# Half-height transposes and a permutation matrix in an attention plus Fourier-mixing kernel on one Trainium2 core

## The chip, the cores and the metric

The kernel runs on one core of one Trainium2 chip. The metric is the device time of one execution in microseconds, the median of several runs. A core has five engines with a queue each: TensorE (PE in the profile; its weight loads are shown apart as PEld), VectorE (DVE), ScalarE (ACT), GpSimd (POOL) and SyncE (SP, which here issues nearly all DMAs). TensorE writes only to PSUM, eight banks of 2 KB in each of 128 partitions; DVE and ACT copy results from there to SBUF.

## The reference

All numbers are 32-bit floats. Two blocks follow each other. The first is linear attention with random features for 8 batches, 8 heads, 576 tokens, head width 64 and 128 features:

```python
def phi(x):
    proj = np.einsum('bhsd,md->bhsm', x, omega)
    sq = np.sum(x * x, axis=-1, keepdims=True) / 2.0
    h = proj - sq
    h = h - np.max(h, axis=-1, keepdims=True)
    return np.exp(h) / np.sqrt(m)
q_p, k_p = (phi(q_s), phi(k_s))
kv = np.einsum('bhsm,bhsd->bhmd', k_p, v)
z = np.sum(k_p, axis=2)
num = np.einsum('bhsm,bhmd->bhsd', q_p, kv)
den = np.einsum('bhsm,bhm->bhs', q_p, z)[..., None] + 1e-06
```

(`num / den` is its result.) The second block takes it as x, 8 x 576 x 512:

```python
X = np.fft.fft(x, axis=1)
X = np.fft.fft(X, axis=2)
mixed = np.real(X).astype(np.float32)
u = x + mixed
mu = np.mean(u, axis=-1, keepdims=True)
var = np.mean((u - mu) ** 2, axis=-1, keepdims=True)
un = (u - mu) / np.sqrt(var + 1e-06)
ch = np.maximum(un @ w_ch1, 0.0) @ w_ch2
return (u + ch).astype(np.float32)
```

## The kernel before, in words

**Two stages.** The first stage does attention, the Fourier mixing of each batch, the conversion of the 64-bit weights to 32-bit floats (`narrow`, L444 to L462), and sums of weight blocks for a Strassen-like scheme (L1326). The second does the two large products, L1501 and L1954, with sums of blocks around them; its first parts (L1658) already run beside the end of the first.

**Attention.** The 64 heads of all batches are taken as 32 pairs, four pairs a batch. Three streams run over the pairs (`pairs`, each takes every third), so that up to three pairs are under way. For one pair (`attn`):

1. The keys and then the queries of two heads are loaded, each 288 KB, to one tile `kq` (L383 and L386). There are two such tiles.
2. `transposed` turns them into `kqT`: nine 128x128 blocks, j = 0 to 8, the first four and a half of which hold keys. Each is one TensorE transpose against the identity (L519). They go in groups of four, four and one, each group to one PSUM bank, and one copy moves a group to SBUF (`evicted`: L535 on ACT or L533 on DVE).
3. `pairs_of` multiplies `kqT` with the random features (L613), for blocks 0 to 3, block 4, and blocks 5 to 8, each time to two neighbouring banks. The first six pairs (`NWIDE`) use tiles of 64 rows and 128 columns, the others tiles of 64 by 64.
4. `softmax` takes the negated maximum on DVE (L556) and the exponential on ACT (L573, 128 columns an instruction, 18 a pair), to tiles `e`. A bank comes free when its last exponential is done.
5. Key features times values give kv (L647, tiles of 64 by 64), kept in SBUF by L661 or L663.
6. `transposed` turns the nine blocks of query features into `qeT` (L519 again), in groups of one, four and four (`ORDER_R` gives the order of the blocks). The copy out of PSUM also moves columns to where the mixing wants its tokens: two copies a group, each reading a strided pattern, six a pair.
7. `qeT` times kv gives numerator and denominator (L694, L702, tiles of 128 rows and 64 columns); DVE forms the reciprocal (L711, L712), and L723 (DVE) or L719 (ACT) the quotient, into one of two token tiles `x`.

**Mixing.** When a batch's four pairs are in `x`, `mix` folds them on DVE or POOL (L750 to L786), multiplies with cosine and sine tables (L806, L816, L856, L867), adds the result to `x` (L913 to L933) and stores `u` to DRAM.

**The order of the work.** Nothing is in the order of the program text. Each piece of work is a `Step` with the engines that may run it and the time that it is thought to take on each; a `Listing` plays the streams forward and always places the step that can begin first on its engine, with small preferences (`bias`). It is greedy; nothing is searched or given by hand. It keeps track of PSUM banks: a step takes a "bank" (one) or a "duo" (two neighbouring ones, an even number first). A step on PE has a `mode`, the tile shape ("whole", "rows", "quarters", "halves"); where it differs from that of the step before, the listing adds 0.12 us. The list that comes out is the order of each engine's queue, and an engine works through its queue in that order, waiting where it must. A whole transpose is priced 0.109 us.

Of the kernel before, what the change touches and what calls it, by code (L numbers as in the profile page):

```python
# [18 lines left out]
F32 = mybir.dt.float32  # L19
# [268 lines left out]
def kernel(  # L288
# [10 lines left out]
    nc = tc.nc  # L299

    B, H, S, D = q.shape
# [14 lines left out]
    R = S // 64  # L316
# [30 lines left out]
    ident = const.tile([128, 128], F32, name="ident")  # L347
# [3 lines left out]
    fix = early.enter_context(tc.tile_pool(name="fix", bufs=1))  # L351
# [7 lines left out]
        kq=NKQ, turned=NS, e=NE, e1=NS, kv=NS, x0=1, x1=1, fold=1, half=1, y=1,  # L359
# [3 lines left out]
    def psum_of(b):  # L363

        i = b.ids[0]
        return banks[:, i] if len(b.ids) == 1 else banks[:, i : i + 2]

    def got():

        return listing.got, psum_of(listing.got)  # L370
# [35 lines left out]
    nc.gpsimd.memset(mhalf[:], -0.5)  # L406
    w2 = hids.tile([128, NFC, DM], F32, name="w2", tag="hid")
    om2 = fix.tile([128, MF], F32, name="om2")


    vds += [fix.tile([P, R, D + 1], F32, name=f"vd{i}") for i in range(NV)]
# [90 lines left out]
    def transposed(src, name, groups, after, makes, give, order=None):  # L502


        dst = None
        for j0, j1 in groups:
            m = j1 - j0
            yield Step(
                PE,
                0.109 * m,  # L510
                after=after(j0, j1),
                take=("bank",) + (("turned",) if j0 == 0 else ()),
                give=give(j0, j1), bias=0.14,
            )
            if dst is None:
                dst = att.tile([128, R, 128], F32, name=name, tag="turned")
            b, ps = got()
            for j in range(j0, j1):
                nc.tensor.transpose(ps[:, (j - j0) * 128 : (j - j0 + 1) * 128], src(j), ident[:])  # L519
            yield Fork(evicted(dst, b, j0, j1, makes, order))  # L520
        return dst

    def evicted(dst, b, j0, j1, makes, order):
        cost = (0.13 + 0.1 * (j1 - j0)) if order else 0.05 + 0.107 * (j1 - j0)
        step = Step(
            {ACT: cost, DVE: 0.06 + 0.133 * (j1 - j0) + (0.06 if order else 0.0)}, late=0.02,
            makes=makes + (j0,), give=(b,), bias=0.08,
        )
        yield step

        def copy(out, in_):
            if step.eng == DVE:
                nc.vector.tensor_copy(out=out, in_=in_)  # L533
            else:
                nc.scalar.activation(out=out, in_=in_, func=AF.Copy)  # L535

        ps = psum_of(b)[:, 0 : 128 * (j1 - j0)].rearrange("q (c p) -> q c p", p=128)
        dst = dst[:, j0:j1, :]
        if order is None:
            copy(dst, ps)  # L540
            return
        h, s, t = order[j0]
        dst = dst.rearrange("q c p -> q (c p)").rearrange("q (h s t c) -> q s h t c", h=h, s=s, t=t)
        ps = ps.rearrange("q c (h t s) -> q s h t c", h=h, s=s)
        for i in range(s):
            of = ps[:, i, :, ::-1, ::-1] if i and j0 else ps[:, i]
            copy(dst[:, i], of)
# [32 lines left out]
    def attn(n):  # L580
        b, pr = divmod(n, NP)

        yield Step(NONE, after=(("k", n),) + ((("vd", n - 1),) if n else ()))
        kq = kqs.pop(n)

        flat = kq[:].rearrange("p c d -> p (c d)")
        kqT = yield from transposed(
            lambda j: flat[:, 128 * j : 128 * j + 128],
            "kqT",
            ((0, 4), (4, 8), (8, R)),  # L590
            lambda j0, j1: (("kq", n),) if j1 > 4 else (),
            ("kqT", n),
            lambda j0, j1: ("kq",) if j1 == R else (),
        )
# [35 lines left out]
        def feature(c):  # L630
# [7 lines left out]
            mode="quarters",  # L638
            after=tuple(("e", n, t) for t in range(3)) + (("vd", n),),
            take=("duo",),  # L640
            give=("e", "e", f"vd{n % NV}"), bias=-0.19,
        )
        kvb, kvp = got()
        for r in range(R):
            for i, h in ((0, 0), (1, 1), (0, 1), (1, 0)):
                rows, cols = slice(D * i, D * i + D), slice(D * h, D * h + D)
# [9 lines left out]
        def keep():  # L656
# [8 lines left out]

        yield Fork(keep())
        qeT = yield from transposed(
            lambda j: feature(R + ORDER_R[j]),
            "qeT",
            ((0, 1), (1, 5), (5, R)),  # L670
            lambda j0, j1: tuple(
                ("e", n, t) for t in sorted({place(R + ORDER_R[j])[0] for j in range(j0, j1)})
            ),
            ("qeT", n),
            lambda j0, j1: {1: ("e1",), 5: (), R: ("e", "e")}[j1],
            {0: (2, 2, 32), 1: (4, 2, 16), 5: (4, 2, 16)},
        )
        yield Step(
# [2 lines left out]
            mode="halves",  # L681
            after=(("kv", n), ("qeT", n, 0), ("qeT", n, 1), ("qeT", n, 5)),
            take=("duo",),
            give=("turned", "kv"), bias=0.12,
# [23 lines left out]
        x = xts[b % 2]  # L708
# [4 lines left out]
        dst = x[:, :, 2 * D * pr : 2 * D * (pr + 1)].rearrange("p c (i d) -> p i c d", i=2)  # L713
        step = Step({DVE: 0.74, ACT: 1.97}, give=(ndb,), makes=("x", b, pr), bias=-0.07)
        yield step
        if step.eng == ACT:
            for i in range(2):
                for c in range(5):
                    nc.scalar.activation(  # L719
                        out=dst[:, i, c], in_=nd[:, i, c, 0:D], func=AF.Copy, scale=rden[:, i, c : c + 1]  # L720
# [3 lines left out]
            out=dst,  # L724
# [270 lines left out]
    turned = {}  # L995
# [421 lines left out]
    def pairs(start):  # L1417
        for n in range(start, B * NP, NS):
            yield from attn(n)
# [770 lines left out]
```

## Time and profile before

| | |
|---|---|
| Time, median of 3 runs (lowest to highest) | 1223.65 us (1218.25 to 1226.66) |
| Time of the profiled execution | 1219.09 us |
| Its span in the profile | 1217.3 us |
| Mean granted clock of TensorE | 0.965 |
| PE, share of the span busy | 92% |
| DVE | 80% |
| ACT | 48% |
| POOL | 23% |

The profile is one execution, taken by the hardware. A line of a group names the line of the kernel, the engine, the operation, what is written and read with shapes (128\*64 is a TensorE tile of 128 rows and 64 columns), the count, the time busy in us with the mean of one in ns, and the idle time just before, with what ended it. A record's length on PE and ACT holds the instruction's latency, so in a row of the same kind the distance from start to start is shorter than the mean, and that distance is what one of them costs. The chain of waits goes back from the last instruction, at each step to what released it, or to the one before it on its engine.

### The profile page before, as it was taken

The numbers are of one execution on the slowest core, as the hardware profiler recorded it, in microseconds if no ns is written. First come the engines' busy times: TensorE is split into PE (matmuls) and PEld (weight loads), VectorE is DVE, ScalarE is ACT, GpSimd is POOL, SyncE is SP. The second block draws the span as 40 slices with busy tenths as digits, with TensorE's granted clock in tenths as the row PEclk, the third lists the DMA queues.
The fourth block names the chain that finished last, engine by engine and source line by source line (L and its number), as shares of the span: only waits on it lengthen the run. The fifth ranks groups of instructions, "written<-read, shape, count | busy, mean of one in ns | idle before, by whom it ended". The sixth has DMA issues, their size and how long they took to land.

```text
span 1217.3 us, 32303 instructions
## 1 busy us (share of the span) xinstructions
PE 1121.6 (92%) x12571; PEld 1034.9 (85%) x12571; DVE 974.1 (80%) x1788; ACT 582.1 (48%) x1795; POOL 276.5 (23%) x292
## 2 busy tenths in 40 slices
PE   8888987987579698999998999999999999999998
PEld 7776876876467588999998988999988999988998
DVE  6998999997878767777877687888867799757895
ACT  7867967967484183261253256322355222332221
POOL 2231332321010120032054125500036400044000
PEclk9998998998798799999999899999999999999999
DMA  9745845848743599898879877875776865757453
GB/s 250 228 143 152 246 119 173 244 136 267 235 162 101 155 312 288 259 288 276 271 224 272 280 245 204 263 202 157 236 210 202 262 183 176 211 150 225 134 156 110
DMA packets 209656, 255.83 MB, mean 210 GB/s; under 512 B 55264, under 2 KB 125152, under 8 KB 209504
## 3 DMA queue, kind: packets, MB, share of 16 engines
q1 hardware_dynamic: 209008, 253.50, 68.4%
q8 instruction: 100, 1.64, 0.6%
q14 instruction: 52, 0.43, 0.1%
q10 hardware_dynamic: 496, 0.26, 0.1%
HBM read 200.74 MB, written 57.15 MB: 212 GB/s over the span
## 4 chain that ended last, share of the span: by engine, by line
PE 76%; DVE 9%; ACT 8%; DMA 5%; issue 1%; SPq 0%; POOL 0%; DVEq 0%; ACTq 0%
PE banks L1954 31%; PE banks L1501 26%; ACT e L573 5%; PE banks L1658 4%; PE banks L613 4%; PE banks L647 3%; PE banks L519 3%; PE banks L694 2%; PE banks L806 2%; DVE nmx L556 2%; DMA wl<-w2l 2%; PE banks L816 1%; DMA raw<-in_moe_w_ch_dram 1%; DVE x L933 1%; ACT qeT L535 1%
## 5 line engine op out<-in xcount | busy, mean ns | idle before, releaser
L1954 PE MATMUL banks<-wl,sums 128*128 128x128 f32 x2016 | 250.4, 278 | 0.7 <-DMA wl<-w2l 0.5
L1954 PEld LDWEIGHTS banks<-wl,sums 128*128 128x128 f32 x2016 | 240.4, 195 | 1.6 <-issue 1.0
L573 ACT ACTIVATE e<-banks,nmx 128x128 f32<-128x128 f32 x576 | 159.3, 443 | 32.7 <-DVE nmx L556 32.7
L1954 PE MATMUL banks<-wl,hid 128*128 128x128 f32 x936 | 122.0, 278 | 8.7 <-DMA wl<-w2l 8.3
L1954 PEld LDWEIGHTS banks<-wl,hid 128*128 128x128 f32 x936 | 113.8, 194 | 9.9 <-issue 4.7
L613 PE MATMUL banks<-om,kqT 64*64 64x128 f32 (+1 forms) x2088 | 91.0, 295 | 29.9 <-ACT e L573 23.7
L613 PEld LDWEIGHTS banks<-om,kqT 64*64 64x64 f32 (+1 forms) x2088 | 75.7, 151 | 41.6 <-ACT e L573 29.3
L556 DVE TENSOR_REDUCE nmx<-banks 128x8 f32<-128x1024 f32 (+1 forms) x96 | 87.3, 951 | 20.4 <-PE banks L613 12.9
L1925 ACT ACTIVATE s<-banks 128x128 f32<-128x128 f32 x126 | 34.9, 277 | 132.9 <-PE banks L1954 116.4
L1501 PE MATMUL banks<-unw,wxw 128*128 128x256 f32 x352 | 85.5, 379 | 0.0
L1954 PE MATMUL banks<-wl,hx 128*128 128x128 f32 x576 | 74.3, 275 | 0.4 <-DVE part L1930 0.4
L1501 PEld LDWEIGHTS banks<-unw,wxw 128*128 128x128 f32 x352 | 66.5, 190 | 8.8
L1930 DVE TENSOR_TENSOR part<-banks,s 128x128 f32<-128x128 f32 x114 | 33.0, 290 | 49.6 <-PE banks L1954 44.4
L1501 PE MATMUL banks<-rx,wxw 128*128 128x256 f32 x288 | 71.1, 379 | 0.0
L1526 ACT ACTIVATE s<-banks 128x512 f32<-128x512 f32 x72 | 42.6, 595 | 57.9 <-PE banks L1501 52.2
L1501 PE MATMUL banks<-ttw,wxw 128*128 128x256 f32 x288 | 70.0, 379 | 0.0
L1954 PEld LDWEIGHTS banks<-wl,hx 128*128 128x128 f32 x576 | 69.4, 192 | 0.7 <-DVE part L1930 0.6
L462 POOL TENSOR_TENSOR w<-w,raw 128x512 f32<-128x512 f32 x30 | 41.4, 1379 | 124.9 <-DVE raw L456 110.3
L1501 PEld LDWEIGHTS banks<-rx,wxw 128*128 128x128 f32 x288 | 54.5, 190 | 7.3
L1501 PEld LDWEIGHTS banks<-ttw,wxw 128*128 128x128 f32 x288 | 54.5, 190 | 7.3
L519 PE MATMUL banks<-ident,kq 128*128 128x128 f32 x288 | 44.8, 296 | 17.0 <-ACT e L573 10.9
L1970 ACT ACTIVATE banks<-banks 128x128 f32<-128x128 f32 x63 | 16.6, 263 | 86.3 <-PE banks L1954 83.9
(244 smaller groups left out, 2398.0 us busy)
## 6 DMA issues: line engine op xcount, KB each, us to landing
wl<-w2l SPq DMA_DIRECT2D x294, 256.0 KB, 3.6
wxw<-w1x SPq DMA_DIRECT2D x120, 256.0 KB, 3.2
raw<-in_moe_w_ch_dram SPq DMA_DIRECT2D x32, 512.0 KB, 5.2
kq<-in_k_dram SPq DMA_DIRECT2D x32, 288.0 KB, 4.0
kq<-in_q_dram SPq DMA_DIRECT2D x32, 288.0 KB, 4.2
vd<-in_v_dram SPq DMA_DIRECT2D x32, 288.0 KB, 4.6
wx<-w1x SPq DMA_DIRECT2D x36, 256.0 KB, 3.3
u<-us SPq DMA_DIRECT2D x128, 64.0 KB, 3.1
```

The source lines that it names most:

```text
L462: eng.tensor_tensor(out=dst, in0=dst, in1=lof, op=ALU.add)
L519: nc.tensor.transpose(ps[:, (j - j0) * 128 : (j - j0 + 1) * 128], src(j), ident[:])
L556: nc.vector.tensor_reduce(nmx[:, :, 0:num], pps[:, :, 0 : MF * num].rearrange("p b (c m) -> p b c m", m=MF), axis=AX.X, op=ALU.max, negate ...
L573: nc.scalar.activation(out=e[:, c + (i if num == 1 else 0), :], in_=pps[:, i, MF * c : MF * c + MF], func=AF.Exp, bias=nmx[:, i, c : c + 1],)
L613: nc.tensor.matmul(pps[cols, c, MF * m : MF * m + MF], lhsT=kqT[rows, j, cols], rhs=om2[rows, :],)
L647: nc.tensor.matmul(kvp[cols, i, 0 : D + 1], lhsT=feature(r)[rows, cols], rhs=vds[n % NV][rows, r, :], start=(r == 0), stop=(r == R - 1),)
L1501: nc.tensor.matmul(ps[:, span * f : span * f + span].rearrange("f (b q) -> f b q", q=Q), lhsT=left[:, P * f : P * f + P], rhs=right, start ...
L1526: nc.scalar.activation(out=s[:], in_=ps, func=AF.Copy)
L1658: nc.tensor.matmul(cell.rearrange("f t (b q) -> f t b q", q=Q), lhsT=w[:, d, col : col + 128], rhs=right[:, :, d].rearrange("f (t b) q -> ...
L1925: nc.scalar.activation(out=s[:], in_=ps[:, 0:128], func=AF.Copy)
L1930: nc.vector.tensor_tensor(out=part[:, t, 128 * m : 128 * m + 128], in0=ps[:, 0:128], in1=saved[with_][:], op=ALU.add,)
L1954: nc.tensor.matmul(ps[:, 0:128], lhsT=left[:, f], rhs=wls[head(j), i, n][:, f], start=start and f == 0, stop=(f == 3), skip_group_check=True,)
```

## The change

In both kinds of transposes eight blocks of nine are done as two half-height tiles each: rows 0 to 63 and rows 64 to 127 of a block are transposed apart, by TensorE tiles of 64 rows, to two neighbouring banks. The ninth stays whole. For this, the steps of a kind are grouped as `(((0, 4), (4, 8)), ((8, R),))`, so the first eight are one step on PE, with mode "rows", priced 0.07 a block, that takes a duo. Its two copies out of PSUM stand in one stream, one behind the other, where before each group's copy was a stream of its own; the duo is given back after the second. The first step of `kqT` now waits for keys and queries, where it waited for the keys alone.

For the query features the identity is replaced by a permutation matrix `perm`, loaded once from DRAM on ACT's queue, and the matmul's output columns are written with strides, so that the columns land in PSUM already in the order wanted. Three plain copies a pair, of 512, 512 and 128 columns, replace the six strided ones.

The diff, without the parts that only rename or regroup:

```diff
+    perm = fix.tile([128, 2, 128], F32, name="perm")
...
+    nc.scalar.dma_start(perm[:], nc.inline_tensor(np.ascontiguousarray(moved_to), name="k_perm").ap())
...
-        for j0, j1 in groups:
+        for parts in groups:
+            j0, j1 = parts[0][0], parts[-1][1]
             m = j1 - j0
+            split = len(parts) > 1
             yield Step(
                 PE,
-                0.109 * m,
+                (0.07 if split else 0.109) * m,
+                mode="rows" if split else "whole",
                 after=after(j0, j1),
-                take=("bank",) + (("turned",) if j0 == 0 else ()),
+                take=("duo" if split else "bank",) + (("turned",) if j0 == 0 else ()),
                 give=give(j0, j1), bias=0.14,
             )
...
+                if order:
+                    i, n = j - j0, (j - j0) // 4
+                    if not split:
+                        nc.tensor.transpose(ps[:, 0:128], src(j), perm[:, 0, :])
+                        continue
+                    for r in range(2):
+                        rows = slice(D * r, D * r + D)
+                        c = i % 4
+                        step_ = 67 - 2 * c
+                        out = ps[:, r, :]
+                        out = bass.AP(out.tensor, out.offset + 256 * n + c, [list(out.ap[0]), [128, 2], [step_, 2], [4, 16]])
+                        nc.tensor.transpose(out, src(j)[rows, :], perm[rows, 1, rows])
+                    continue
+                if split:
+                    for r in range(2):
+                        rows = slice(D * r, D * r + D)
+                        nc.tensor.transpose(
+                            ps[:, r, (j - j0) * D : (j - j0 + 1) * D], src(j)[rows, :], ident[rows, rows]
+                        )
+                    continue
                 nc.tensor.transpose(ps[:, (j - j0) * 128 : (j - j0 + 1) * 128], src(j), ident[:])
-            yield Fork(evicted(dst, b, j0, j1, makes, order))
+            yield Fork(evicted(dst, b, parts, makes, order))
...
+    def evicted(dst, b, parts, makes, order):
+        for j0, j1 in parts:
+            yield from copied(dst, b, j0, j1, parts, makes, order)
...
-            makes=makes + (j0,), give=(b,), bias=0.08,
+            makes=makes + (j0,), give=(b,) if j1 == parts[-1][1] else (), bias=0.08,
...
+        if order and split:
+            k0 = D * (j0 - parts[0][0])
+            copy(dst.rearrange("q c p -> q (c p)").rearrange("q (r x) -> q r x", r=2), psum_of(b)[:, :, k0 : k0 + 256])
+            return
+        if order:
+            copy(dst[:, 0, :], psum_of(b)[:, 0:128])
+            return
+        if split:
+            k0 = D * (j0 - parts[0][0])
+            ps = psum_of(b)[:, :, k0 : k0 + D * (j1 - j0)].rearrange("q r (c p) -> q c r p", p=D)
+            copy(dst.rearrange("q c (r p) -> q c r p", r=2), ps)
+            return
...
-            ((0, 4), (4, 8), (8, R)),
-            lambda j0, j1: (("kq", n),) if j1 > 4 else (),
+            (((0, 4), (4, 8)), ((8, R),)),
+            lambda j0, j1: (("kq", n),),
...
-            ((0, 1), (1, 5), (5, R)),
+            (((0, 1),), ((1, 5), (5, R))),
```

More of the change, by code (lines that the diff above doesn't have):

```diff
@@ L408 @@
     om2 = fix.tile([128, MF], F32, name="om2")
+    perm = fix.tile([128, 2, 128], F32, name="perm")
+    h_, s_, t_ = np.meshgrid(np.arange(2), np.arange(2), np.arange(32), indexing="ij")
+    told = [(h_ * 64 + t_ * 2 + s_).ravel()]
+    h_, s_, t_ = np.meshgrid(np.arange(4), np.arange(2), np.arange(16), indexing="ij")
+    told.append((h_ * 32 + np.where(s_ == 1, 15 - t_, t_) * 2 + s_).ravel())
+    moved_to = np.stack([np.eye(128, dtype=np.float32)[:, o] for o in told], axis=1)
+    nc.scalar.dma_start(perm[:], nc.inline_tensor(np.ascontiguousarray(moved_to), name="k_perm").ap())
     vds += [fix.tile([P, R, D + 1], F32, name=f"vd{i}") for i in range(NV)]
@@ L518, in transposed, with copied @@
             for j in range(j0, j1):
+                if order:
[18 more added lines that the diff above has]
+                    continue
                 nc.tensor.transpose(ps[:, (j - j0) * 128 : (j - j0 + 1) * 128], src(j), ident[:])
-            yield Fork(evicted(dst, b, j0, j1, makes, order))
+            yield Fork(evicted(dst, b, parts, makes, order))
         return dst
-    def evicted(dst, b, j0, j1, makes, order):
+    def evicted(dst, b, parts, makes, order):
+        for j0, j1 in parts:
+            yield from copied(dst, b, j0, j1, parts, makes, order)
+    def copied(dst, b, j0, j1, parts, makes, order):
+        split = len(parts) > 1
         cost = (0.13 + 0.1 * (j1 - j0)) if order else 0.05 + 0.107 * (j1 - j0)
@@ L535, in copy @@
                 nc.scalar.activation(out=out, in_=in_, func=AF.Copy)
+        dst = dst[:, j0:j1, :]
+        if order and split:
[10 more added lines that the diff above has]
+            return
         ps = psum_of(b)[:, 0 : 128 * (j1 - j0)].rearrange("q (c p) -> q c p", p=128)
-        dst = dst[:, j0:j1, :]
         if order is None:
@@ L674, in attn @@
             ("qeT", n),
-            lambda j0, j1: {1: ("e1",), 5: (), R: ("e", "e")}[j1],
+            lambda j0, j1: {1: ("e1",), R: ("e", "e")}[j1],
             {0: (2, 2, 32), 1: (4, 2, 16), 5: (4, 2, 16)},
```

## The prediction

> **What bounds the kernel now.** I read the page first (busy shares, slices), then the table by stage, then the chain of waits up to 412 us, the waits of the same stretch, and last single records of the transposes in the timeline.
>
> The table by stage, cut where the last attention and mixing work ends (columns: length, PE, PEld, DVE, ACT, POOL busy with counts, granted clock, DMA share, GB/s):
>
> ```profile
> 0.00:412.00 412.00, 340.75 (x6923) 291.62 (x6923) 351.75 (x683) 293.60 (x1091) 98.38 (x86) 0.93 0.61 184
> 412.00:1217.30 805.30, 780.83 (x5648) 743.30 (x5648) 622.40 (x1106) 288.46 (x705) 178.10 (x206) 0.98 0.73 224
> ```
>
> All that the change touches lies in the first 412 us. No engine is the bound there: DVE is busy 85%, PE 83%, ACT 71%. The rest is PE at 97% and holds no changed instruction; it can only start earlier or later.
>
> Groups of that stage (busy us, mean ns | idle before):
>
> ```profile
> L573 ACT ACTIVATE e<-banks,nmx 128x128 f32<-128x128 f32 x576 | 159.3, 443 | 32.7 <-DVE nmx L556 32.7
> L519 PE MATMUL banks<-ident,kq 128*128 128x128 f32 x288 | 44.8, 296 | 17.0 <-ACT e L573 10.9 <-DVE x L723 5.3 <-ACT kqT L535 0.4
> L519 PE MATMUL banks<-ident,e 128*128 128x128 f32 x288 | 42.9, 282 | 2.3 <-ACT e L573 1.6 <-issue 0.4
> L535 ACT ACTIVATE qeT<-banks 128x256 f32<-128x256 f32 x124 | 39.5, 450 | 1.1 <-PE banks L519 0.7
> L535 ACT ACTIVATE kqT<-banks 128x512 f32<-128x512 f32 x57 | 33.9, 655 | 4.2 <-PE banks L519 3.9
> L613 PE MATMUL banks<-om,kqT 64*128 64x128 f32 x216 | 15.3, 281 | 0.5 <-ACT kqT L535 0.3 <-ACT e L573 0.2
> ```
>
> 576 transposes are 9 of each kind in 32 head pairs. A pair's query features leave PSUM in six copies (two of 64 columns, four of 256), 31 pairs' on ACT.
>
> Waits up to 412 us (total, times, longest):
>
> ```profile
> ACT e L573 <- DVE nmx L556: 32.7, 19, 4.9
> PE banks L613 <- ACT e L573: 23.7, 14, 2.9
> PE banks L519 <- ACT e L573: 12.5, 11, 4.5
> ```
>
> Scores and key/query transposes read nothing of e: those waits are for PSUM banks that the exponentials still hold. So three engines hand the stage round. Summing the chain's pieces up to 412 us gives PE 191.4, DVE 96.8, ACT 90.4, DMA 14.3, issue 15.0; in it L519 holds 31.3, e L573 58.3, qeT copies 9.9, kqT copies 9.9. These shares convert engine time into path time below.
>
> Two neighbouring segments on PE:
>
> ```profile
> 259.11 2.18 PE L519 MATMUL banks<-ident,e 128*128 128x128 f32 x18
> 261.22 1.15 PE L694 MATMUL banks<-kv,qeT 128*64 128x65 f32 x32
> 261.22 1.01 PEld L694 LDWEIGHTS banks<-kv,qeT 128*64 128x64 f32 x32 [0.17 <-issue]
> ```
>
> Read record by record, whole transposes start 109 ns apart; the next segment, another tile shape, loads 202 ns after the last one's start, and its first matmul waits for its load. L694's two half-width tiles run side by side: a slot of two takes 59 ns for 65 moving columns.
>
> **The change part by part.**
>
> *Transposes on PE.* Before, a segment of nine costs 9 x 109 + 149 = 1130 ns (149: 93 for the change of tile shape and 56 for the first load, from the records above). After, eight become two 64-row tiles each, with 64 moving columns, and one stays whole. The nearest row with 64 moving columns is L694's slot, 59 ns; that two row tiles run side by side is shown by L613 64*128, whose slots of two with 128 columns are 112 ns apart. So a segment is 8 x 59 + 149 = 621, and the whole one, now a segment of its own, 109 + 149 = 258. That is 879 against 1130, and for 64 segments -16.1 us of PE. Two pairs' segments that now merge still merge (rows with rows), so the difference is the same. Bounds: if each whole one finds a neighbour of its own shape, its 149 goes and 64 x 0.149 = 9.5 more is saved: -25.6. If a slot can't go under 109 because of the load, the segment is 1021 + 258 = 1279: +9.5. I take -16.1, since the load records support it: a transpose's 128-column load lasts 140 ns, L694's load 138, and L694's go through in 59 ns slots. On the path: L519 has 31.3 us of chain for 64 x 1.13 = 72.3 us of segments, 43%; -16.1 x 0.43 = -7.0 us (ends -11.0 and +4.1).
>
> [...] No run before shows a 64x128 load under 64 moving columns.
>
> *Strided writes of the query features.* Matmuls now write PSUM every fourth column. L856 writes every second one: its records start 110 to 112 ns apart, as do unstrided ones of its width. Taken 0; at worst twice the slot, 8 x 59 x 32 = +15.1 us of PE, 43% of it +6.5.
>
> *Copies.* On ACT, starts in a row are 264 ns apart for 256 strided columns, 104 for 64, 478 for 512, 157 for 128. Six copies: 4 x 264 + 2 x 104 = 1264; three: 2 x 478 + 157 = 1113. Times 31: -4.7 us of ACT. The chain holds 9.9 of 31 x 1.264 = 39.2, 25%: -1.2 us. The key/query copies keep their sizes and read 64-column runs out of two banks; the strided 256-column copy costs what y's plainer one does (264), so 0. Bounds: at best -2.4 us (half on the path), at worst, if a second bank costs a start of 50 ns (from 478 - 4 x 107), 128 x 0.05 x 0.25 = +1.6.
>
> *Two banks at once.* The eight transposes take an aligned pair where they took two single banks, one after the other. Exponentials free a pair's two banks one step (four of them, 1.0 us) apart, so the first four transposes can no longer start on the first. Queued behind a waiting transpose on PE are scores, kv and mixing products of other streams. But the second group needed its bank anyway; what is lost is the four transposes' 0.44 us, unless the pair is broken by a single elsewhere. The row has 11 such waits: 11 x 0.44 x 0.43 = +2.1 us taken; none is the lower end, a full step at each of 64 takings on the path (+27) the upper.
>
> *Query load.* The first key/query segment now waits for q too. Its DMA is issued 0.45 us after k's; a first landing at 1.17 + 3.9 = 5.1 against a start at 4.36 costs 0.7 once; there a transpose takes 0.22 us (nine in 2.02), twice the later one, so the segment's saving of 0.25 doubles to 0.5: +0.2. Later loads are issued 20 us ahead: 0, and nothing about that if cover fails but the same 0.7 each.
>
> *Permutation matrix.* 128 KB on ACT's queue, issued once (0.48 us as om's), before the table load; ACT first works at 5.46 after 2.9 idle: hidden, and 128 KB at the 350 GB/s of these first us could push q by 0.4.
>
> *Order.* The listing is made afresh from steps priced 0.07 a transpose plus 0.12 a change of shape (0.68 against 0.62 here). A pair's two copies are now one stream, one behind the other. In which place raw loads (11.0 us of chain) and maximum reductions fall can't be worked out; the same bank wait before L613 returns at 62.99, 155.45 and 247.25, so the order repeats every two batches and a different repeat counts four times: 3 us either way is 12. I take 0.
>
> Sum: -7.0 - 1.2 + 2.1 + 0.2 = -5.9. The profiled execution took 1219.1 (span 1217.3 plus 1.8), so 1213.2; it stands 4.6 under the median 1223.65, so 1217.8, say 1218.
>
> **The rivals.**
> 1. *The order falls well*: whole transposes merge with mixing products, PE's ends count fully: -25.6 x 0.43 - 2.4, and a repeat shorter by 1 to 3 us: 1198 to 1210. For it: 208 changes of tile shape before 412 us, many beside whole products. Against: each stream's single transpose lies between its own other shapes.
> 2. *Hidden anyway*: PE waits longer for banks, since exponentials (159 us of ACT) and reductions set the pace: 36.2 us of PE's waits are theirs already. Then only the copies and 0 count: 1222 to 1226.
> 3. *Pairs of banks* (the other side): transposes and scores both want aligned pairs, and singles break them. Price 1.0 us a wait for one more exponential step; it decides from the point where 6 of 64 takings more than I counted wait on the path, and with 25 of them it gives 1243. For it: 23.7 us of L613's waits are just such. Against: singles were three a segment before and are one now.
> 4. *Loads bind*: slot 109: +4.1 in place of -7.0, 1229. Against: L694's slots. [...]
>
> **How the numbers follow.** Forecast 1211 to 1222: 0.35. Rival 1: 0.25. Rival 2: 0.13. Rival 3: 0.20, most of it over 1236. Rival 4: 0.07. About 1% is what a measurement of this kernel tells from no change, 1211.4 to 1235.9 here. Faster: rival 1, 0.25, and the forecast's edge 0.01: 0.26. Slower: 0.17 of rival 3. Same: 0.57. Range: from inside rival 1 (1200, 0.07 left below) to inside rival 3 (1243, 0.09 left above). The likeliest case's own range is 1211 to 1222.
>
> **What would show it.** In the profile after: L519 64*128 records in slots near 59 ns (109: rival 4); ACT's query copies at three a pair and some 35 us by their starts in place of 39; L519's and L613's waits on e L573, 36.2 us in sum: about the same in the forecast, longer by 10 or more with an unchanged end in rival 2, longer with a later end in rival 3. The last mixing work should end near 406 instead of 412. If this point moves and the end does not, DMA waits of the second stage have eaten it. An end of stage off by more than 10 us with slots and copies as worked out means the order decided, and my zero for it was the wrong step.

## The result and the profile after

The changed kernel takes 1227.35 us (median of 18 runs, 1218.92 to 1231.0); the kernel before, on the same chip, takes 1221.99 us (18 runs). The ratio, worked out from all runs (the two medians alone would give 1.0044), is 1.0038, with a 95% interval of 1.0021 to 1.0055: no change by the prediction's bound of about 1%, but by the ratio 4.6 us slower, where 5.9 us faster was forecast. The profiled execution took 1224.86 us, its span is 1223.1 us, and the mean granted clock is 0.948 where it was 0.965.

The table by stage of the kernel after, cut at the same point as before:

```profile
0.00:412.00 412.00, 333.87 (x7413) 284.80 (x7413) 341.47 (x668) 278.48 (x956) 92.06 (x90) 0.89 0.61 183
412.00:1223.10 811.10, 783.28 (x5672) 744.56 (x5671) 626.16 (x1120) 289.81 (x712) 178.81 (x208) 0.98 0.74 223
```

In the first 412 us PE is busy 6.9 us less and ACT 15.1 us less, and yet the stage became longer: its last mixing products end at 413.5 us, before at 409.0. The number that moved the wrong way is the granted clock: 0.93 before, 0.89 now. The second stage has its 0.98 as before.

Groups of that stage in the kernel after (lines are shifted: exponentials are L620, query transposes L540 and L532, key/query transposes L545 and L549, copies L570, kv products L694, quotients' products L741):

```profile
L620 ACT ACTIVATE e<-banks,nmx 128x128 f32<-128x128 f32 x576 | 158.4, 450 | 43.6 <-DVE nmx L603 43.5
L694 PE MATMUL banks<-vd,e 64*64 64x65 f32 x2304 | 51.8, 251 | 5.2 <-DVE kqT L568 2.0 <-ACT kqT L570 1.8 <-ACT e L620 0.9
L741 PE MATMUL banks<-kv,qeT 128*64 128x65 f32 x1024 | 44.0, 248 | 7.0 <-ACT e L620 2.0 <-ACT bmp L953 1.7 <-ACT qeT L570 1.7
L570 ACT ACTIVATE kqT<-banks 128x512 f32<-128x512 f32 x59 | 35.8, 645 | 11.7 <-PE banks L545 11.4
L570 ACT ACTIVATE qeT<-banks 128x512 f32<-128x512 f32 x57 | 33.7, 636 | 5.4 <-PE banks L540 5.4
L545 PE MATMUL banks<-ident,kq 64*128 64x64 f32 x512 | 26.3, 247 | 10.7 <-ACT e L620 4.8 <-DVE x L770 4.7 <-ACT x L766 0.6
L540 PE MATMUL banks<-perm,e 64*128 64x64 f32 x512 | 25.1, 242 | 10.9 <-ACT e L620 9.1 <-ACT qeT L570 1.2 <-DVE qeT L568 0.6
```

The strided writes (L540) are no dearer than the plain ones (L545): a record is 242 ns long against 247. Waits of the same stretch in the kernel after:

```profile
ACT e L620 <- DVE nmx L603: 43.5, 21, 4.3
PE banks L540 <- ACT e L620: 9.1, 6, 1.9
PE banks L660 <- ACT e L620: 7.9, 7, 1.7
PE banks L545 <- ACT e L620: 4.8, 3, 3.8
```

The waits on e of scores (L660) and transposes, 36.2 us before, are 23.7 us now, with 1.9 us of the ninth key/query transposes (L549). So neither "hidden anyway" nor "pairs of banks" describes what happened: both had these waits grow. One pair's query transposes in the kernel after:

```profile
389.46 0.33 PE L532 MATMUL banks<-perm,e 128*128 128x128 f32 x1
389.72 0.72 PE L540 MATMUL banks<-perm,e 64*128 64x64 f32 x16
```

Sixteen half-height transposes go through as eight slots of two, 62 ns from start to start at full clock, read record by record; only the first slot of a segment (in some the second) takes 112. 59 was predicted.

Last, the clock in 40 slices of the span (tenths of full speed), in the kernel after:

```profile
PEclk9899998897879599899999899999999999999999
```

The lowest digits (7, 7, 5) are those of slices 10, 12 and 14, between 275 and 428 us. Counted from the profile's clock records up to 520 us, the changed kernel spends 119.5 us at half clock and the one before 78.5 us. One stretch alone, from 396.7 to 430.8 us, is 34.1 us long; before, the longest there is 13.7 us (412.8 to 426.4).

### The profile page after: what moved, and what is told of

Read it like the earlier page. It is cut to its first block, busy times and chain, and to the rows that moved or that the text cites. A ratio compares the mean times of both kernels' runs of the same rounds, so it can differ in the third digit from the quotient of the medians.

```text
span 1223.1 us, 33174 instructions
## 1 busy us (share of the span) xinstructions
PE 1117.2 (91%) x13083; PEld 1029.4 (84%) x13083; DVE 967.6 (79%) x1787; ACT 568.3 (46%) x1668; POOL 270.9 (22%) x297
## 4 chain that ended last, share of the span: by engine, by line
PE 61%; DMA 3%; DVE 2%; issue 0%; SPq 0%; ACT 0%; DVEq 0%
PE banks L2001 31%; PE banks L1548 27%; PE banks L1705 3%; DMA wl<-w2l 3%; DVE ttw L1345 0%; DVE w1s L1451 0%; DVE unxw L1242 0%; DVE rx L1504 0%; DMA us<-x 0%; SPq L994 0%; DVE unw L1242 0%; DVE so L1504 0%; DVE hid L1591 0%; DVE unw L1345 0%; DVE rx L1242 0%
## 5 line engine op out<-in xcount | busy, mean ns | idle before, releaser
L620 ACT ACTIVATE e<-banks,nmx 128x128 f32<-128x128 f32 x576 | 158.4, 450 | 43.6 <-DVE nmx L603 43.5
L660 PE MATMUL banks<-om,kqT 64*64 64x128 f32 (+1 forms) x2088 | 80.3, 280 | 19.3 <-ACT e L620 7.9
L660 PEld LDWEIGHTS banks<-om,kqT 64*64 64x64 f32 (+1 forms) x2088 | 68.2, 143 | 28.8 <-ACT e L620 10.3
L694 PE MATMUL banks<-vd,e 64*64 64x65 f32 x2304 | 51.8, 251 | 5.2 <-DVE kqT L568 2.0
```

Of the source, the lines that this page charges most:

```text
L620: nc.scalar.activation(out=e[:, c + (i if num == 1 else 0), :], in_=pps[:, i, MF * c : MF * c + MF], func=AF.Exp, bias=nmx[:, i, c : c + 1],)
L660: nc.tensor.matmul(pps[cols, c, MF * m : MF * m + MF], lhsT=kqT[rows, j, cols], rhs=om2[rows, :],)
L694: nc.tensor.matmul(kvp[cols, i, 0 : D + 1], lhsT=feature(r)[rows, cols], rhs=vds[n % NV][rows, r, :], start=(r == 0), stop=(r == R - 1),)
```

## The experiments

Every kernel is compared with the kernel before on its own chip. Of two of them, the ratio is the quotient of their ratios, and its interval the two half-widths as root of the sum of squares. "Half clock" is the time at half clock up to 520 us in the profiled execution; that is one execution of each kernel, so the mean clock of all runs is given below as well.

**First question: order, copies or tiles?** One theory (A) had the tiles save what was worked out and the new order take it back. The other (B) had the saving hidden, with the order at fault again. Two kernels keep the changed kernel's listing, step by step, and put other operations in its places.

`old_ops_new_order`: whole transposes against the identity for both kinds, and two strided copies a group of query features.

```diff
-   for r in range(2): nc.tensor.transpose(<64-row half of src(j)>)
+   nc.tensor.transpose(ps[:, n, 128 * c : 128 * c + 128], src(j), ident[:])
...
-   copy(<512 plain columns>)
+   copy(<256 strided columns>); copy(<256 strided columns>)
```

> The changed kernel with its listing untouched (same steps, prices, banks, so the same order of work), but with the old operations in it: whole transposes against the identity, and two strided copies a group of query features. Theory A (the half-height tiles and the plain copies save the 6 to 8 us worked out in the prediction, and the new order of the listing costs about 11): 1232 to 1236 us, some 7 over the changed kernel. Theory B (the saving is hidden behind other engines, and the order costs the 4 to 5 us): within 1.5 us of the changed kernel, 1226 to 1229.

Measured: 1218.68 us, 0.9961 (0.9937 to 0.9986). The new order, with its pairs of banks and its copies in one stream, is better than the old one, by 0.4% or about 5 us. Theories A and B both needed it to be worse.

`whole_tiles_new_order`: the same listing, the permutation matrix and plain copies stay, and only the half height is undone. (The copies of `kqT` then read one bank each instead of two; on ACT they last 652 ns on average, in the changed kernel 645.)

```diff
-   for r in range(2):
-       nc.tensor.transpose(<half out>, src(j)[rows, :], perm[rows, 1, rows])
+   out = bass.AP(out.tensor, out.offset + c, [list(out.ap[0]), [128, 4], [67 - 2 * c, 2], [4, 16]])
+   nc.tensor.transpose(out, src(j), perm[:, 1, :])
```

> The changed kernel with its listing untouched, but each transpose is whole: one tile of 128 rows, the permutation matrix still there for the query features with strided output columns, three plain copies a pair. Against the changed kernel only the half-height tiles are undone. Theory A: 5 to 7 us over the changed kernel, and 1 to 2 under the one with the old operations. Theory B: the same as both within 1.5 us.

Measured: 1217.22 us, 0.9956 (0.9936 to 0.9976). Against `old_ops_new_order` the permutation and plain copies are worth 0.05% plus or minus 0.32%, nothing that can be told. Against the changed kernel this says where the loss is: in the same order, half-height tiles cost 0.82% (0.56 to 1.08), about 10 us, though each segment of them is cheaper. Theories A and B are both wrong.

The first stage of this kernel in the table by stage, its clock in 40 slices, and the two groups that do the same work as L694 and L741 above:

```profile
0.00:412.00 412.00, 339.41 (x6923) 291.40 (x6923) 347.76 (x683) 280.55 (x964) 92.30 (x91) 0.93 0.61 186
```

```profile
PEclk9899999998889799999999999999999999999999
```

```profile
L681 PE MATMUL banks<-vd,e 64*64 64x65 f32 x2304 | 47.1, 235 | 3.5 <-DVE kqT L561 1.6 <-ACT kqT L563 1.0 <-ACT e L607 0.9
L728 PE MATMUL banks<-kv,qeT 128*64 128x65 f32 x1024 | 41.2, 235 | 4.8 <-ACT e L607 1.9 <-DVE bmp L959 1.2 <-ACT qeT L563 0.9
```

PE is busy 5.5 us longer here in 412 us, and the clock is 0.93 instead of 0.89 (half clock 71.7 us). The same 2304 kv products take 47.1 us where the changed kernel needs 51.8, and the 1024 products behind them 41.2 against 44.0. Nothing about these instructions differs but when they run.

As the order is the same, the two traces can be laid upon each other, instruction by instruction. Taken at the exponentials on ACT, the delay of the changed kernel is 0 until 25 us, 1.6 at 37 us, 0.4 at 100, 1.8 at 150 and 1.2 at 210 us. It is 3.7 at 230 us, 3.4 at 300 and 5.8 at 364; at the first cosine product of the last batch it is still 5.8, after the last mixing 8.7, and no more after that. The first step, in the timeline of PE in the changed kernel and in this one:

```profile
25.59 2.00 PE L741 MATMUL banks<-kv,qeT 128*64 128x65 f32 x32 [1.53 <-DVE qeT L568]
...
27.81 1.95 PE L741 MATMUL banks<-kv,qeT 128*64 128x65 f32 x32
...
30.12 1.87 PE L694 MATMUL banks<-vd,e 64*64 64x65 f32 x72
```

```profile
26.83 1.09 PE L728 MATMUL banks<-kv,qeT 128*64 128x65 f32 x30
...
28.14 1.28 PE L681 MATMUL banks<-vd,e 64*64 64x65 f32 x72
```

The changed kernel does its transposes sooner, then waits 1.53 us for a copy, and has half clock from 24.6 to 31.4 us (6.8 us): 72 kv products in 1.87 us instead of 1.28. The step at 222 us goes with half clock from 215.8 (6.8 us), which the other has not. The last step is the mixing of the last batch, in the changed kernel:

```profile
398.14 2.50 PE L853 MATMUL banks<-cs_sb,fold 128*128 128x160 f32 x8 [5.15 <-DVE fold L826]
400.57 1.44 PE L863 MATMUL banks<-cs_sb,fold 64*128 64x320 f32 x4
402.40 2.50 PE L853 MATMUL banks<-sn_sb,fold 128*128 128x160 f32 x8 [0.39 <-DVE fold L826]
404.84 1.44 PE L863 MATMUL banks<-sn_sb,fold 64*128 64x320 f32 x4
406.76 1.23 PE L903 MATMUL banks<-sd_sb,y 128*128 128x129 f32 x4 [0.48 <-ACT y L876]
```

and with whole tiles:

```profile
392.30 2.50 PE L840 MATMUL banks<-cs_sb,fold 128*128 128x160 f32 x8 [5.15 <-DVE fold L813]
394.73 1.44 PE L850 MATMUL banks<-cs_sb,fold 64*128 64x320 f32 x4
396.56 2.22 PE L840 MATMUL banks<-sn_sb,fold 128*128 128x160 f32 x8 [0.39 <-DVE fold L813]
398.71 0.81 PE L850 MATMUL banks<-sn_sb,fold 64*128 64x320 f32 x4
400.00 0.71 PE L890 MATMUL banks<-sd_sb,y 128*128 128x129 f32 x4 [0.48 <-ACT y L863]
```

Both begin at half clock, after 5.15 us of waiting for DVE's folds. With whole tiles full clock is back at 398.4 us, and the same four sine products take 0.81 us instead of 1.44. In the changed kernel it stays away until 430.8. That costs 3 us between the first cosine product (5.8 us late) and the second product's first matmul (8.7 us late).

These are single executions. In the profile of `half_tiles_warm_end` below, whose instructions are the same up to 392 us, the delay is 0.3 us at 36 us, 3.8 at 204, 6.0 at 232 and 5.7 at the first cosine product: the steps lie elsewhere, and the sum up to the last mixing is the same. Nor does the long half clock at the end come with every such wait: from the first cosine product to the last product the changed kernel takes 15.4 us, the five other profiled kernels with the same wait there (5.15 or 5.16 us) 11.0 to 12.5 us, `half_tiles_filled` below among them.

So a third theory: the saving turns into idle time of PE, the chip grants half clock for longer, and that costs more than was saved. Its rival is that the row tiles themselves cost something that the records don't show.

**The first products in front of the last pair.** In the changed kernel, L1705 (the first large product, which nobody waits for yet) stands ahead of the last pair's products:

```profile
377.20 8.90 PE L1705 MATMUL banks<-unT,w 128*128 128x256 f32 x40
...
386.93 1.15 PE L741 MATMUL banks<-kv,qeT 128*64 128x65 f32 x32
```

The greedy listing filled a gap that, on the chip, wasn't one. `after_held` and `before_held` hold these products back until the last batch is in `x`, so that they fall into the waits of its mixing instead:

```diff
-        yield Step(NONE, after=("w2 done",))
+        yield Step(NONE, after=("w2 done",) + tuple(("x", B - 1, pr) for pr in range(NP)))
```

> The changed kernel, with the first weight products (the block of 40 matmuls that PE runs from 377 to 386 us ahead of the last pair's product) held until the last batch's four pairs are in x. Theory A with the loss at the end of the stage: the last batch's cosine product starts near 390 us in place of 398, and the time falls by 5 to 9 us, to 1218 to 1222. Rival (the loss is spread over the stage, the tail only hides it): the time stays within 2 us of the changed kernel, or rises, since PE then has nothing to do while it waits.

> The kernel before with the same hold. There the last pairs were through PE at 378.6 us, ahead of the first products that run from 382 us. Theory A: nothing to gain, within 2 us of the kernel before, or up to 4 slower. Rival (first products hinder attention in general): faster by as much as the changed kernel with the hold.

Measured: `after_held` 1216.18 us, 0.9928 (0.9902 to 0.9954), 1.1% or some 13 us under the changed kernel, where 5 to 9 us were expected, with half clock at 92.2 us. The order on PE is the changed kernel's until 369 us, so it is the hold that brings this. `before_held` 0.9999 (0.9974 to 1.0024). Before, the last pairs were through at 378.6 us, and nothing stood in front of them. This defect belongs to the new order, and the whole tiles have it too.

`whole_tiles_held`, the same in the kernel with whole tiles:

> Whole transposes in the new order, and the first weight products held until the last batch's pairs are in x. If the two effects are separate, the gain of the hold (some 11 us on the changed kernel) or the part of it that is not clock (5) comes on top of the 0.9956 of the whole tiles: 1206 to 1213 us. If the hold only repaired the clock at the end of the changed kernel's stage (34 us of half clock there, 20 here), it brings 2 us or less: 1215 to 1218.

Measured: 1208.99 us, 0.9889 (0.9859 to 0.9918). The hold is worth 0.7% here, and half-height tiles still cost 0.4% (plus or minus 0.4%).

**Is it the clock?** `half_tiles_filled` and `whole_tiles_filled` put useless work where PE was relieved: four more whole transposes of the identity behind each ninth block, 28 us of PE in all.

```diff
+            if not split:
+                for i in range(4):
+                    nc.tensor.transpose(ps[:, 128 + 128 * (i % 3) : 256 + 128 * (i % 3)], ident[:], ident[:])
```

> The changed kernel, listing untouched, with useless work added to PE: four whole transposes of the identity behind each ninth block, to columns of its bank that nobody reads (256 matmuls of 0.109 us, 28 us of PE, a little more than the half-height tiles had saved). Clock theory (the half-height tiles cost time because a PE that is busy less is granted half the clock more often): in spite of the added work it falls back towards the whole tiles, 1217 to 1222, and half clock before 520 us falls from 119 to about 75 us. Rival (the half-height tiles cost time through their banks, their changes of shape or later copies): the added work comes on top, 1230 to 1240, with half clock of some 75 to 119 us making no difference.

> The same useless work behind each ninth block in the kernel with whole transposes in the new order. It shows what the added work costs by itself. Clock theory: half clock before 520 us falls below the 72 us there, and the time changes little, 1215 to 1222. Rival: the work is paid where PE is on the path, some 43% of 28 us, 1227 to 1231.

Measured: half-height tiles with it 1227.52 us, 1.0038 (1.0017 to 1.0058), the same as without; whole tiles 1227.34 us, 1.0030 (1.0009 to 1.0051), 0.7% more than without. Half clock goes from 119.5 to 88.7 us in the one and from 71.7 to 58.0 us in the other. 28 us of extra work cost the changed kernel nothing, and with it half height and whole height are level (1.0008, plus or minus 0.0029). The rival, a hidden cost of the row tiles, should have left the 0.8% between them. By their numbers, though, the clock theory missed both times: it expected 1217 to 1222 and 1215 to 1222 us. With whole tiles the added work costs 9 us, as the rival had it (1227 to 1231). So the pair speaks for the clock by its difference alone, and it doesn't exclude that the added work falls into waits that the row tiles themselves make.

`whole_tiles_two_left_out` tests the other direction: whole tiles, but two of the eight blocks of each segment are not transposed, 14 us less of PE with no row tile in the kernel. The copies keep their lengths and take other blocks' columns twice, so the output is not the reference's.

```diff
+                    if c == 3:
+                        continue
```

> Whole transposes in the new order, listing untouched, but of the eight blocks of a kind the fourth and the eighth are left out (the copies keep their lengths and take the other blocks' columns twice), so the features of those blocks are not the reference's. This takes 2 x 0.109 = 0.22 us a segment off PE, 14 us in all, as much as the half-height tiles took off (1.13 to 0.90), without any tile of 64 rows. Clock theory (any PE time saved here is paid back in granted clock): the clock falls from 0.967 towards 0.955 and the time does not fall by the 7 us that the work is worth, 1214 to 1224. Rival (it is the 64-row tiles that lower the clock or cost time): the clock stays at 0.967 and the time falls to 1208 to 1212.

Measured: 1216.78 us, 0.9952 (0.9926 to 0.9978), level with the 0.9956 of all blocks; by the prediction's 43% it should have been 6 us faster. Its first stage:

```profile
0.00:412.00 412.00, 335.80 (x6795) 285.24 (x6795) 344.64 (x678) 280.07 (x964) 92.46 (x91) 0.91 0.60 184
```

The clock fell from 0.93 to 0.91 (half clock 95.6 us, 71.7 with all blocks). So PE work that is taken away here comes back as lower clock with whole tiles too. It did not cost 10 us, though, as the half-height tiles do.

The profile shows one thing more. The last exponential is 5.7 us later than with all blocks, as late as in the changed kernel, and the first cosine product of the last batch starts at 397.7 us (398.1 in the changed kernel, 392.3 with all blocks). So the delay along the stage can build up with no row tile at all, though this is one execution, at 1220.02 us some 3 us over the median. The last mixing then takes 11.0 us, not 15.4.

`half_tiles_warm_end` leaves the changed kernel as it is and gives PE useless matmuls in its last waits: 18 before the last cosine products, 4 before the sine products, 80 before the first second-stage product. (In the trace the 18 leave 36 records and the 4 leave 8.)

```diff
+            for _ in range((18, 4)[n] if b == B - 1 else 0):
+                nc.tensor.matmul(yp[:, 0, 0:128], lhsT=zeros[:], rhs=zeros[:], start=True, stop=True, skip_group_check=True)
...
+        for _ in range(80 if i == len(CLEAN) - 1 else 0):
+            nc.tensor.matmul(ps[:, 0:256], lhsT=eye[:, 0:128], rhs=eye, start=True, stop=True, skip_group_check=True)
```

> The changed kernel with useless matmuls where PE waits at the end of the first stage: 18 ahead of the last batch's cosine product (PE idles there for 5 us), 4 ahead of its sine product, 80 small ones ahead of the first weight products that wait for DVE (11 us idle). They read constants only, so nothing that is waited for gets work to do. Clock theory: the 34 us of half clock from 397 to 431 us shrink to some 10, the last mixing runs at full clock, and the time falls by 3 to 7 us, to 1220 to 1224. Rival (the low clock only goes with the waits and costs nothing): within 2 us of 1227, or slower by what the useless work adds.

Measured: 1218.92 us, 0.9970 (0.9950 to 0.9990): work that nobody needs makes the changed kernel 0.7% faster, 8 us. The last mixing in its timeline:

```profile
392.78 4.29 PE L851 MATMUL banks<-zeros 128*128 128x128 f32 x36
398.00 1.35 PE L855 MATMUL banks<-cs_sb,fold 128*128 128x160 f32 x8 [0.94 <-DVE fold L826]
399.28 0.81 PE L865 MATMUL banks<-cs_sb,fold 64*128 64x320 f32 x4
...
404.96 0.71 PE L905 MATMUL banks<-sd_sb,y 128*128 128x129 f32 x4 [0.48 <-ACT y L878]
```

It starts at 398.0 us as it did without, and the eight cosine products take 1.35 us instead of 2.50. The table by stage from 380 to 440 us, first of the changed kernel, then of this one:

```profile
380.00:440.00 60.00, 41.84 (x345) 33.87 (x344) 40.48 (x84) 14.12 (x38) 6.97 (x5) 0.72 0.48 155
```

```profile
380.00:440.00 60.00, 52.78 (x495) 44.76 (x493) 41.21 (x86) 18.81 (x48) 10.18 (x11) 1.00 0.56 181
```

`whole_tiles_warm_end` is the same with whole tiles:

> Whole transposes in the new order with the useless matmuls at the end of the stage (18, 4 and 80), as the half-height tiles had them. Half clock at the end is 20 us here (34 there). If all that the half-height tiles lose is lost at the end, both come out alike with the end kept warm: 1216 to 1220, the warm end bringing 1 us or less. If they also lose along the stage, by the half clock of 3.4 to 7 us at a time that shifts them step by step to 5.8 us by 380 us, the whole tiles gain at the end as well, and stay 3 to 6 us ahead: 1212 to 1216.

Measured: 1215.16 us, 0.9938 (0.9914 to 0.9961), 0.2% better than without, plus or minus 0.3%. The difference between the tiles falls from 0.82% to 0.32% (0.01 to 0.63). So some 6 of the 10 us go with the waits at the end of the stage, and some 4 stay; the split is rough, as either difference is known to 0.3% only. In the two profiles with a warm end, the half-height tiles are 5.3 us behind at the first cosine product and 2.8 us at the end of the span: what is left lies ahead of the last mixing.

Over all runs, and not the profiled ones alone, the mean granted clock is 0.950 in the changed kernel and 0.969 with whole tiles. With the filling it is 0.962 and 0.972, with the warm end 0.963 and 0.977, and with two blocks left out 0.963. So the lower clock of the half-height tiles is no accident of one profile, and they lower it more than the blocks left out do.

**How far does the order alone scatter?** The kernel before, all operations as they were, with another price of a whole transpose in the listing (`0.109 * m` becomes `0.118 * m`, then `0.100 * m`):

> The kernel before, every operation as it was, with one number of the listing changed: a whole transpose is priced 0.118 us in place of 0.109. It shows how far the greedy order alone moves the time. If an order is worth what the steps in it are worth, within 2 us of the kernel before. If the order scatters, as the 0.4% that the new order gave with the old operations suggests, anything within 8 us either way.

> The kernel before with a whole transpose priced 0.100 us in place of 0.109, every operation as it was. A second draw from the greedy orders: the first, at 0.118, was 0.5% slower, with an almost wholly different list. If orders scatter, anything from 1214 to 1232; if the listing is best at the true price (109 ns in the records), slower than before again, 1225 to 1231.

Measured: 1.0051 (1.0030 to 1.0071) and 1.0130 (1.0097 to 1.0163). One number in the listing can move the time by more than any part of this change.

**The best version.** Hold and useless matmuls together (14, 4 and 80 of them), with whole and with half-height tiles:

> Whole transposes in the new order, first weight products held, and the same useless matmuls at the end of the stage (14, 4 and 80). There first products already fill the last mixing's waits, and what is left is 14 us of half clock from 406 us, about 5 us of it under work of PE. Clock theory: 1 to 3 us faster than without them, 1205 to 1209. Rival: no change or 1 to 4 slower, the 18 matmuls ahead of the last mixing being in its way.

> The changed kernel with the first weight products held and the warm end (14, 4 and 80). With whole tiles the two gave 0.9875. If the loss is all at the end, the half-height tiles now give the same or better, 1203 to 1208. If they lose along the stage too, they stay 3 to 7 us behind, 1210 to 1215.

Measured: whole tiles 1207.68 us, 0.9875 (0.9845 to 0.9905), which beats both kernels; half-height tiles 1213.6 us, 0.9923 (0.9896 to 0.9950). The useless matmuls add nothing that can be told to the hold alone (0.9889 and 0.9928), which has put other work into the same waits. Half clock is 51.2 and 92.2 us. Half height still costs 0.5% (0.1 to 0.9), with the end of the stage warm in both. In these profiles the first cosine product starts at 383.3 and 390.7 us: this part lies earlier.

## Why the prediction was wrong

The range held the time and "no change by 1%" was the likeliest verdict, but the sign was wrong. By its steps:

- *Price of a segment*: right. Slots are 62 ns (59 predicted), after a segment's first one of 112. At half clock they are 107 ns. The rival "loads bind" falls: at full clock the load records of the half-height transposes are 139 ns long, and two of them start in each slot of 62 ns, so their length doesn't set the slots.
- *Transposes on the path, -7.0 us*: this is the step that failed. It took the clock as given and converted saved PE time into path time by a share of the chain. In the same order the half-height tiles cost +10 us (0.82%), where -7.0 was forecast. What the runs show in its place is the clock: with PE's saved time idle it is granted less (0.950 over all runs against 0.969 with whole tiles), and useless matmuls in the last waits give 8 us back. The blocks left out show that saved PE time can be taken back whole; that the tiles lose 10 us on top is explained for some 6 of them, by the end of the stage, and open for the rest. No rival had this, though the table by stage of before showed a clock of 0.93 in the one stage where PE isn't full.
- *Order, 0*: a gain of 5 us (0.4%). The 12 us that the prediction gave either way are about what repricing one step makes (+0.5% and +1.3%), so the size of the unknown was right and its sign could not be worked out.
- *Copies, -1.2 us*: nothing measurable (0.05%, plus or minus 0.32%, or 4 us), an interval that holds -1.2 as well as 0. That the strided writes cost nothing is shown by their slots, 63 ns on the median against 62 for the plain ones.
- *Two banks at once, +2.1 us*: not seen apart from the order; PE's waits on e fell from 36.2 to 23.7 us in a stage that ends later.
- *Last mixing near 406 instead of 412*: its last products end at 413.5 us, where they ended at 409.0; 6 us earlier was predicted.

The sum of what was measured, -0.4% for the order, 0 for the copies and +0.8% for the tiles, is the +0.4% of the result, as it must be, since each is a quotient of neighbouring kernels.

What stays open: the 4 us that remain with the end kept warm. In the traces, delay steps at 25 and 222 us go with half-clock stretches that only the changed kernel has; in another execution of the same instructions the steps lie elsewhere, and no run warmed such places one by one. Whether every run of the changed kernel has the 34 us of half clock at the end isn't known either, as only one was traced. And whether the matmuls of 64 rows lower the clock by themselves wasn't separated from idle time: two blocks left out saved about as much PE work as the tiles do, lowered the clock less (0.963 against 0.950) and cost nothing, while the tiles cost 10 us.

## What to carry to other kernels

Before crediting a saving on an engine that isn't the bound of its stage, look at the granted clock of that stage: where it is under full speed already (0.93 here), PE time saved may come back as idle time at half clock (0.89 here), and useless matmuls in the longest waits may be worth more than the saving (8 us here, where the saving was forecast at 7.0). Where a greedy listing makes the order, test an edit with the order held fixed, and reprice one step to learn how far the order alone scatters. Idle stretches just ahead of a serial tail (here the last batch's mixing) cost most in this kernel (some 6 of the 10 us): the eight cosine products behind the 5.15 us wait took 2.50 us, and 1.35 where useless matmuls had taken up all but 0.94 us of that wait.

## What the hardware showed

In the clock records of the two profiles, before and after, the granted clock is 0.5 or 1.0, and the stretches at half clock last 3.4, 6.8, 10.2, 13.7 or 34.1 us. Long gaps were not needed for it: the changed kernel has half clock from 24.6 us on, after waits of PE of 0.40 and 0.56 us and 0.5 us into one of 1.53 us. Added transposes kept the clock up: 28 us of them cut the half clock from 119.5 to 88.7 us in the changed kernel and raised the mean clock of all runs from 0.950 to 0.962; with whole tiles they cut it from 71.7 to 58.0 us, and the mean clock rose from 0.969 to 0.972.

Over the 18 runs of the changed kernel, the time goes with the mean clock (correlation -0.87): 1230.7 us at 0.944, 1219 at 0.958.
